# Three-stage chain on one core: steps of the second block on other tiles, a difference of x behind the last low part, one conversion fewer behind a product

## The chip, the cores and the metric

The kernel runs on one core of a Trainium2 chip. The metric is device time in microseconds (us). Before the change three runs gave a median of 1089.61 us, with 1087.82 as the lowest and 1091.75 as the highest.

## The reference

Three stages follow each other; the output of one is the input of the next.

```python
# 1: retention, 4 x 8 heads, 768 steps, head size 64
state = gamma * state + outer(k[t], v[t]);  y[t] = scale * q[t] @ state
x = y as 3072 tokens x 512
# 2: first MLP, w_in 512 x 2048, w_out 2048 x 512
h = maximum(x @ w_in, 0);  x = (h * h) @ w_out
# 3: second MLP, w_gate and w_val 512 x 1536, w_out 1536 x 512
xn = x / sqrt(mean(x * x) + 1e-6) * rms_g
out = (silu(xn @ w_gate) * (xn @ w_val)) @ w_out
```

All of it is float32 on the outside.

## The kernel before, in words

A product of two float32 matrices is made of three TensorE passes over operands that are split in two: a high part (ScalarE casts to fp32r, L105, L339, L488) and a low part (VectorE subtracts the high part from the value, L102). The weights of the later token blocks are used in the form of seven combinations of their four quarters (P1 to P7), so that seven products stand for eight. Such a combination is called a unit here: VectorE adds or subtracts quarters (`plus`, L112, and `sub`, L109), `put` splits the result into high and low part, and SyncE's queue stores it to device memory (L162, `ui` for w_in and `uo` for w_out), from where a ring of tiles fetches it again (L441, `more_ring` and its like).

The 3072 tokens go through the kernel in blocks of 512. Blocks 0 and 1 use the plain weights; block 1 is the **second block** that the change speaks of (`block1(1, ...)`). It walks over 16 tiles f = 0 to 15 of the hidden size. In each tile TensorE multiplies x by w_in (`proj`, L323), ScalarE makes relu, its square and the high part (r L336, r L337, s L339), VectorE makes the low part of s (L102), and TensorE multiplies s by w_out one tile later (`tail1`, `out1`, L281 to L283). On every even tile TensorE also does a **visit** of the retention: one chunk of 128 tokens, with the products for the state and the values (L982, L993, L1002) and the scores of the next chunk (L947). A visit needs q of the next chunk multiplied by its decay on GpSimd (`decay_q`, L924), and q comes from device memory just before (L902).

After block 1 blocks 2 and 3 run as one pair with the combined weights; the pair goes over groups n of four hidden tiles, and over the products k in each group in the order P1, P2, P6, P5, P7, P3, P4 (`after1(n, k)` is called behind each product; visits are behind P6 and P3). The operands of x for these products are made by `first_x` from raw x (three `sub` of 128x1024 and seven `put`).

Three generators are advanced by hand with `next()`, one step at a time, at fixed tiles:

- `made` makes the units of w_out: two steps that add high and low part of four tiles again (`whole_rows`), then `plus` and `sub`, `put(P5)`, `sub` with `put(P7)`, `sub` with `put(P6)`, `put(P3)`.
- `made_in` makes the units of w_in in the same way.
- `coming_xs` is `first_x`.

Beside them a **tick** takes one tile of a later weight of stage 3 a step further: ScalarE unpacks a raw tile into f (L232, L235), VectorE finishes it (L246), SyncE stores the tile before (L205) or a low part is made, and SyncE fetches the next raw tile (L221, 512 KB). `more_steps` opens this list and fetches the first three raw tiles; in block 1 it is called in `last1` at f = MORE_AT.

Nothing is scheduled by a tool: the order of the program's calls is the order on each engine. Within one tile of block 1 that order is `early1`, the background step, `proj`, r/r/s on ScalarE, `late1`, the visit, the mask on VectorE (L965, L970), the low part of s, `after_visit` (copies L314, state L112 and L1013, loads of q, k and v), the decays on GpSimd, `last1`, and `tail1`. All DMAs shown here are issued by SyncE in that order. Working tiles come from one pool of 38 slots (`slot()`), so a write into a slot waits for the last use of it, and that use can be the store of an earlier unit.

Of the kernel before, what the change touches and what calls it, by code (L numbers as in the profile page):

```python
# [35 lines left out]
NF1, NF2 = FF1 // 128, FF2 // 128  # L36
# [4 lines left out]
COMING = (0, 1, 2, 5, 8, 9, 13, 16, 17, 18, 19, 20)  # L41
AHEAD = 5
EARLY = 24
MORE_AT = 6
W2_SOON = 25
X_AT = (11, 12, 17, 18, 23, 24)

P2, P1, P5, P6, P7, P3, P4 = range(7)
# [12 lines left out]
def retention_then_two_mlps(  # L61
# [27 lines left out]
    def slot(name, dt=F32):  # L89
        return wp.tile([128, 2, 512], dt, tag="w", name=name)  # L90

    def big(name, dt=F32):
        return xp.tile([128, KC, TB], dt, tag="x", name=name)
# [10 lines left out]
    def split(dst_h, dst_l, src, el):  # L104
        nc.scalar.copy(dst_h, src)  # L105
        low(el, dst_l, src, dst_h)

    def sub(out_, a, b, eng=nc.vector):
        eng.tensor_tensor(out=out_, in0=a, in1=b, op=ALU.subtract)  # L109
# [144 lines left out]
    def stores():  # L254
        while later:
            later.pop(0)()

    def tick(low_first=False, ahead=True):
        i = at[0]
        rest_of = None  # L260
        if i - 1 in done:
            fn, key, _ = steps[i - 1]
            rest_of = fn(key, done.pop(i - 1))
        if i < upto[0]:
            magnitude(i)
            if ahead:
                magnitude(i + 1)
        if low_first and rest_of:
            rest_of()
        if i < upto[0]:  # L270
            convert(i)
            at[0] = i + 1
        if not low_first and rest_of:
            rest_of()

    def more_steps(n):
        upto[0] = min(upto[0] + n, len(steps))
        fetch_to(at[0] + 2)
# [50 lines left out]
    def background():  # L329
        for w in back[:]:  # L330
            if next(w, StopIteration) is StopIteration:
                back.remove(w)
# [259 lines left out]
    def first_x(raws):  # L592
        y = {(h, t): raws[t].t[:, 2 * h:2 * h + 2, :] for h in range(2) for t in range(2)}

        def put(k, src, wide=False):
            if wide:
                t = big("xop", F32R)
                X[k] = [t[:, 0:2], t[:, 2:4]]
            else:
                X[k] = [slot("xop", F32R) for _ in range(2)]  # L600
            split(*X[k], src, nc.vector)

        yield
        put(P1, y[0, 0])
        yield
        put(P2, y[1, 0])
        yield
        put(P3, y[1, 1])
        yield
        sub(y[0, 0], y[0, 1], y[0, 0])  # L610
        sub(y[0, 1], y[1, 1], y[0, 1])
        yield
        sub(y[1, 1], y[1, 1], y[0, 0])
        yield
        put(P6, y[1, 1])
        yield
        put(P5, y[0, 0])
        yield
        put(P7, y[0, 1], True)
        yield  # L620
        sub(y[1, 0], y[1, 0], y[1, 1])
        put(P4, y[1, 0], True)
        yield
# [242 lines left out]
    with tc.manual_schedule():  # L866
# [92 lines left out]
        def mask(first=0):  # L959
            if not masks:  # L960
                return
            P, sc = masks.pop()
            for h in (first, 1 - first):
                o, i = (a.rearrange("p (g e) i -> p g e i", g=2)[..., D:] for a in (P[:, h], sc[h]))
                nc.vector.tensor_tensor(  # L965
                    out=o, in0=i, in1=seen_sb[:, :, D:].unsqueeze(2).to_broadcast([128, 2, 2, D]), op=ALU.mult
                )
                for n, b in enumerate(heads):
                    g = slice(2 * n, 2 * n + 2)
                    nc.vector.tensor_tensor(  # L970
                        out=P[b, h, g, :D], in0=sc[h][b, g, :D],
                        in1=seen_sb[b, n, :D].unsqueeze(1).to_broadcast([D, 2, D]), op=ALU.mult,
                    )
# [54 lines left out]
        def visit(c, next_banks, with_sums, also=None):  # L1028
            kv = into_state(c)
            kv0 = into_state(also, pr[0]) if also else None  # L1030
            if with_sums:
                sums(pr[0][:, 2 * C:])
            values(c, halves())
            scores(c + 1, next_banks)
            return kv, kv0

        def after_visit(c, x, kv):
            x.put(columns_of(c), halves())
            take_state(c, kv)
            load(c + 2)  # L1040
            load_q(c + 2)
            load_k(c + 2)
            load_v(c + 2)
# [140 lines left out]
        def tail1():  # L1184
            nonlocal prev
            if prev is None:
                return
            pf, s, pj = prev
            prev = None
            out1(pf, s)  # L1190
            if pf == NF1 - 1:
                back.append(norm1(pj, 2 + 2 * pj))
                next(back[-1])
# [76 lines left out]
        def keep_out(f):  # L1270
            keep_units(uo, f, W[("o", f)])

        def keep_in(f):
            q, r, m = f // 4, f % 4 // 2, f % 2
            w = W[("i", f)].bitcast(F32)
            for k, h in ((P1, 0), (P2, 1)) if r == 0 else ((P4, 1),):
                nc.sync.dma_start(units(ui[q][k])[:, m], w[:, :, h * HALF:(h + 1) * HALF])
# [32 lines left out]
        coming_xs = None  # L1310

        def sink1(c):
            nonlocal coming_xs
            t = c // B - 2
            if t == len(raws1):
                raws1.append(Raw())
                if t:
                    coming_xs = first_x(raws1)
                    next(coming_xs)
            return raws1[t]  # L1320

        def early1(f):
            if f in (1, 2, 3, 4, 5, 6, 7, 9, 13):
                next(made)
            if f == NF1 - 1:
                next(coming_xs)

        def late1(f):
            if f + NF1 - 5 < NF1:
                keep_out(f + NF1 - 5)  # L1330
            if f + 4 < NF1:
                keep_in(f + 4)
            if f == NF1 - 1:
                next(coming_xs)
            if f % 2 and 1 < f < NF1 - 1:
                next(made_in)
            elif f == 1:
                next(made)

        def more_ring():  # L1340
            n = len(ring)
            ring.append(slot(f"ring{n}", F32R))
            nc.sync.dma_start(ring[n].bitcast(F32), stream[n])
# [3 lines left out]
        def last1(f):  # L1347
            stores()
            if f >= RING_AT:
                more_ring()  # L1350
            if f < 8 or f in (12, 13):
                next(made)
            if f == MORE_AT:
                more_steps(W2_SOON)
            if f > MORE_AT and f % 2:
                tick(ahead=False)
            if 2 <= f < NF1 - 1:
                next(made_in)
            if f in (8, 10, 14, 15):
                next(coming_xs)  # L1360

        block1(1, cur, sink1, (0, 2, 4, 6, 8, 10, 12, 14), early1, late1, last1)
        stores()
        making_1 = chain(made_in, made)
# [3 lines left out]
        def sink2(c):  # L1368
            t = c // B - 4
            if t == len(xs2):  # L1370
                xs2.append(Raw())
            return xs2[t]
# [18 lines left out]
        def next_chunk():  # L1391
            nonlocal at_chunk
            decay_v(at_chunk + 1, nc.gpsimd)
            decay_q(at_chunk + 2, nc.gpsimd)
            at_chunk += 1

        def after1(n, k):
            if (n, k) == (0, P1):
                tail1()
            else:  # L1400
                background()
            mask()
            stores()
            at_step = k in (P2, P5, P4) or (n, k) == (2, P1)
            if at_step:
                tick(ahead=False)
            if k == P5 or k == P4 and n < NQ - 1:
                next_chunk()
            if k in (P6, P3):
                kv, _ = visit(at_chunk, (ph, pb)[(n + 1) % 2] if k == P6 else pa, True)  # L1410
                after_visit(at_chunk, sink2(at_chunk), kv)
            if at_step:
                next(making_1, None)
            if n == 0 and k in (P1, P2, P6):
                next(coming_xs)
            if (n, k) == (0, P1):
                more_ring()
            if n == NQ - 1 and k in (P2, P6, P3):
                i = (P2, P6, P3).index(k)
                out_1.hi(i)  # L1420
                out_1.lo(i)

        for n in range(NQ):
            in_pair(n, after1)
# [318 lines left out]
```

## Time and profile before

| what | value |
| --- | --- |
| median of three runs | 1089.61 us (1087.82 to 1091.75) |
| the profiled execution's own time | 1087.85 us |
| its span in the profile | 1086.1 us |
| granted TensorE clock, mean | 1.000 of full speed |
| busy share: PE, DVE, ACT, POOL | 99%, 72%, 55%, 7% |

The profile gives the busy time of each engine: PE is TensorE's matmuls, DVE VectorE, ACT ScalarE, POOL GpSimd and SPq SyncE's queue, which issues the DMAs. Times inside the trace count from the start of the span. The span is 1.75 us shorter than the execution's own time. Since PE is busy for 99% of it, the time is that of TensorE's work and of the few places where it waits.

### The profile page before, as it was taken

Reading aid. Unit: us, or ns where it says so; the run is one execution under the profiler, and the core shown is the slowest. Engines: PE = TensorE matmul, PEld = TensorE weight load, DVE = VectorE, ACT = ScalarE, POOL = GpSimd, SP = SyncE. Lnnn points to the kernel's source line nnn. Section 1 sums busy time; section 2 is a strip of 40 time slices with the busy share of each in tenths; the row PEclk is TensorE's granted clock in tenths of the full one; section 3 lists DMA queues with packets and bytes.
Section 4 is the critical chain, followed back from the end, with each engine's and each line's share of the span. In section 5 each row is a group of like instructions: output and inputs, shape, how many; then the busy total and the mean of one; then the engine's idle time right before and its main releaser. Section 6 shows DMA issues by size and latency. Waiting matters only on the chain. (4 is left out here: it accounts for less than half of the span.)

```text
span 1086.1 us, 16642 instructions
## 1 busy us (share of the span) xinstructions
PE 1075.8 (99%) x6257; PEld 883.8 (81%) x6257; DVE 785.3 (72%) x1078; ACT 592.5 (55%) x913; POOL 74.3 (7%) x65
## 2 busy tenths in 40 slices
PE   9999999999999999999999999999999999999998
PEld 7788887878878788888887887888888888888887
DVE  6988698796758995579788887995333896433585
ACT  5777445667677649885465555453333554233442
POOL 3000142214210000000000000000000000000000
PEclk9999999999999999999999999999999999999999
DMA  9979899999999979987669979767567667555563
GB/s 362 339 241 354 260 319 354 383 388 405 344 372 353 348 273 384 388 271 239 200 227 335 378 280 364 263 212 238 194 230 253 194 212 252 194 194 194 194 213 117
DMA packets 110180, 307.16 MB, mean 283 GB/s; under 512 B 11236, under 2 KB 34556, under 8 KB 110100
## 3 DMA queue, kind: packets, MB, share of 16 engines
q1 hardware_dynamic: 109920, 305.85, 79.1%
q8 instruction: 50, 0.82, 0.3%
q10 hardware_dynamic: 180, 0.24, 0.1%
q14 instruction: 30, 0.25, 0.1%
HBM read 217.43 MB, written 88.62 MB: 282 GB/s over the span
## 5 line engine op out<-in xcount | busy, mean ns | idle before, releaser
L488 ACT CAST o<-act 128x1024 fp32r<-128x1024 f32 x101 | 105.6, 1052 | 110.1 <-DVE act L109 50.1
L102 DVE TENSOR_TENSOR o<-act,o 128x1024 fp32r<-128x1024 f32 x101 | 123.0, 1222 | 26.6 <-ACT o L488 26.5
L282 PE MATMUL ph<-o,ring 128*128 128x512 f32 x228 | 88.8, 389 | 0.0
L281 PE MATMUL ph<-o,ring 128*128 128x512 f32 x228 | 88.5, 388 | 0.0
L283 PE MATMUL ph<-o,ring 128*128 128x512 f32 x228 | 88.5, 388 | 0.0
L109 DVE TENSOR_TENSOR act<-act 128x1024 f32<-128x1024 f32 x68 | 83.0, 1221 | 0.3
L281 PE MATMUL ph<-xop,ring 128*128 128x512 f32 x208 | 81.5, 392 | 0.8 <-ACT part L116 0.7
L281 PE MATMUL pb<-xop,ring 128*128 128x512 f32 x208 | 81.4, 391 | 0.4 <-ACT part L116 0.3
L281 PE MATMUL pa<-xop,ring 128*128 128x512 f32 x208 | 81.4, 391 | 0.0
L323 PE MATMUL ph<-xh,w_i 128*128 128x512 f32 x248 | 81.0, 390 | 0.0
L283 PE MATMUL pb<-xop,ring 128*128 128x512 f32 x208 | 81.0, 389 | 0.0
L282 PE MATMUL ph<-xop,ring 128*128 128x512 f32 x208 | 81.0, 389 | 0.0
L283 PE MATMUL pa<-xop,ring 128*128 128x512 f32 x208 | 80.9, 389 | 0.0
L283 PE MATMUL ph<-xop,ring 128*128 128x512 f32 x208 | 80.9, 389 | 0.0
L282 PE MATMUL pb<-xop,ring 128*128 128x512 f32 x208 | 80.9, 389 | 0.0
L282 PE MATMUL pa<-xop,ring 128*128 128x512 f32 x208 | 80.9, 389 | 0.0
L112 DVE TENSOR_TENSOR part<-pr,part 128x512 f32<-128x512 f32 x38 | 25.7, 689 | 52.5 <-ACT part L116 51.2
L760 ACT ACTIVATE t<-part 128x512 f32<-128x512 f32 x54 | 34.1, 632 | 50.0 <-DVE part L112 50.0
L116 ACT COPY part<-ph 128x512 f32<-128x512 f32 x52 | 29.9, 588 | 52.3 <-PE ph L283 52.3
L323 PEld LDWEIGHTS ph<-xh,w_i 128*128 128x128 f32 x248 | 46.5, 188 | 10.2 <-ACT w_o L136 0.4
L282 PEld LDWEIGHTS ph<-o,ring 128*128 128x128 f32 x228 | 42.8, 188 | 9.6 <-DVE o L102 0.9
L281 PEld LDWEIGHTS ph<-o,ring 128*128 128x128 f32 x228 | 42.8, 188 | 9.1 <-issue 0.2
(251 smaller groups left out, 2597.7 us busy)
## 6 DMA issues: line engine op xcount, KB each, us to landing
ring<-wu SPq DMA_DIRECT2D x84, 512.0 KB, 3.9
ring<-up SPq DMA_DIRECT2D x63, 512.0 KB, 4.3
ring<-ui SPq DMA_DIRECT2D x56, 512.0 KB, 6.6
ring<-uo SPq DMA_DIRECT2D x56, 512.0 KB, 4.9
wu<-ring SPq DMA_DIRECT2D x42, 512.0 KB, 7.0
raw<-w1i SPq DMA_DIRECT2D x16, 512.0 KB, 6.9
raw<-w1o SPq DMA_DIRECT2D x16, 512.0 KB, 6.9
vkt<-vk SPq DMA_DIRECT2D x16, 512.0 KB, 7.1
```

The costliest lines, as they stand in the source:

```text
L102: eng.tensor_tensor(out=dst_l, in0=src, in1=dst_h.bitcast(F32), op=ALU.subtract)
L109: eng.tensor_tensor(out=out_, in0=a, in1=b, op=ALU.subtract)
L112: eng.tensor_tensor(out=out_, in0=a, in1=b, op=ALU.add)
L116: nc.scalar.copy(dst[:, m], acc[m])
L281: nc.tensor.matmul(acc, ah, bh, start=start, stop=False, **more)
L282: nc.tensor.matmul(acc, ah, bl, start=False, stop=False, **more)
L283: nc.tensor.matmul(acc, al, bh, start=False, stop=stop, **more)
L323: nc.tensor.matmul(h, w[:, a, k * 128:(k + 1) * 128], x[b][k], start=n == 0, stop=n == len(order) - 1)
L488: nc.scalar.copy(h, src)
L760: nc.scalar.activation(t, g, AF.Silu)
```

## The change

Five places are edited, all in the order of the work; the arithmetic is the same.

```diff
-MORE_AT = 6
+MORE_AT = 4
...
 # first_x
         sub(y[1, 1], y[1, 1], y[0, 0])
-        yield
         put(P6, y[1, 1])
...
         def early1(f):
-            if f in (1, 2, 3, 4, 5, 6, 7, 9, 13):
+            if f in (0, 1, 2, 5, 6, 7, 11, 12, 13):
                 next(made)
...
 # late1
-            if f == NF1 - 1:
-                next(coming_xs)
...
 # last1
             if f > MORE_AT and f % 2:
                 tick(ahead=False)
-            if 2 <= f < NF1 - 1:
+            if 1 <= f < NF1 - 2:
                 next(made_in)
...
 # after1
             at_step = k in (P2, P5, P4) or (n, k) == (2, P1)
-            if at_step:
+            if at_step and k != P1:
                 tick(ahead=False)
```

Three steps of `made` move (from f = 3, 4 and 9 to f = 0, 11 and 12), all steps of `made_in` in `last1` come one tile earlier, the first raw tiles are fetched two tiles earlier and a tick is added at f = 5, the third difference of x leaves the f = 15 code ahead of the low part, and the tick behind the third group's first product goes. The number of steps and of ticks over the whole kernel is the same. From the third group's second product on, the order on all engines is that of before.

Below, rows are shown as they stand in program order on one engine, before and now. Line numbers of the changed kernel are one lower from L614 on.

**ScalarE, second block, from the square of tile 5 to that of tile 6** (r_1988 and r_1992 are tile 5's relu, r_2042 and r_2054 tile 6's; made tiles are units). Before:

```order
L337 ACTIVATE r_1988<-r_1988 128x512 [waits Activation_49]
L339 CAST s_1991<-r_1988 128x512 [waits DMAHW1_49,Activation_49]
L105 CAST made_1996<-rows_1803 128x2x256
L105 CAST made_2006<-rows_1850 128x2x256 [waits DVE_49]
L105 CAST made_2010<-sm_1854 128x2x256 [waits DVE_49,PE_49]
L105 CAST made_2026<-sm_1950 128x2x256 [waits DVE_49]
L336 ACTIVATE r_2042<-ph0_230 128x512 [waits PE_49]
```

Now:

```order
L337 ACTIVATE r_1992<-r_1992 128x512 [waits Activation_49]
L339 CAST s_1995<-r_1992 128x512 [waits Activation_49]
L105 CAST made_2000<-sm_1846 128x2x256 [waits DVE_49]
L105 CAST made_2008<-sm_1976 128x2x256 [waits DMAHW1_49,DVE_49]
L232 ACTIVATE rows_2015<-raw_1954 128x512 [waits DMAHW2_49]
L235 ACTIVATE raw_1954<-raw_1954 128x512 [waits DMAHW4_49]
L105 CAST made_2022<-rows_1707 128x2x256 [waits DMAHW0_49,DVE_49]
L105 CAST made_2038<-rows_1853 128x2x256 [waits DVE_49]
L336 ACTIVATE r_2054<-ph0_230 128x512 [waits PE_49]
```

The four casts ahead of tile 6's relu are still four, the added tick puts L232 and L235 among them, and the third cast, made_2022, now also waits for a DMA: its slot is the one that made_2000 had, and the DMA is the store of made_2000 (`ui03<-made_2000`).

**VectorE, second block, tile 5, between the state's addition and the mask of tile 6.** Now:

```order
L112 TENSOR_TENSOR rows_1854<-w_o6_895 128x512 [waits DMAHW7_49]
L112 TENSOR_TENSOR rows_1854<-w_o7_944 128x512
L109 TENSOR_TENSOR sm_1846<-sm_1846,rows_1707 128x512 [waits DVE_49]
L102 TENSOR_TENSOR made_1961<-rows_1708,made_1961 128x2x256 [waits Activation_49]
L112 TENSOR_TENSOR sm_1976<-rows_1853,rows_1854 128x512 [waits DMAHW1_49,DVE_49]
L109 TENSOR_TENSOR rows_1853<-rows_1853 128x2x256 [waits DVE_49]
L109 TENSOR_TENSOR rows_1707<-rows_1707,sm_1846 128x2x256
L102 TENSOR_TENSOR made_2000<-sm_1846,made_2000 128x2x256 [waits PE_49,Activation_49]
L102 TENSOR_TENSOR s_1995<-r_1992,s_1995 128x512
```

Before, six instructions of the same size stood between the state's addition and tile 5's low part of s; now eight do, the last of them the low part of made_2000. Between the state's addition of the visit before (f = 2) and the mask of f = 4 there were 14 such instructions and are nine now.

**VectorE, second block, tile 15** (raw is x for `first_x`, xop its split operands). Before, and behind it now:

```order
L102 TENSOR_TENSOR xop<-raw,xop 128x1024
L109 TENSOR_TENSOR raw<-raw 128x1024 x3
L102 TENSOR_TENSOR s<-r,s 128x512
L102 TENSOR_TENSOR wps<-rows,wps 128x512
L246 SCALAR_TENSOR_TENSOR f<-f,raw 128x512
L102 TENSOR_TENSOR xop<-raw,xop 128x1024
```

```order
L102 TENSOR_TENSOR xop<-raw,xop 128x1024
L109 TENSOR_TENSOR raw<-raw 128x1024 x2
L102 TENSOR_TENSOR s<-r,s 128x512
L246 SCALAR_TENSOR_TENSOR f<-f,raw 128x512
L109 TENSOR_TENSOR raw<-raw 128x1024
L102 TENSOR_TENSOR xop<-raw,xop 128x1024
```

The third difference moved from ahead of the low part of s to behind it.

## Rows read from the trace of the kernel before

**Rows 1.** The page, part 1: busy time, share, instructions of each engine.

```profile
PE 1075.8 (99%) x6257; PEld 883.8 (81%) x6257; DVE 785.3 (72%) x1078; ACT 592.5 (55%) x913; POOL 74.3 (7%) x65
```

**Rows 2.** PE's waits: line, what ended them, us in total, times, longest.

```profile
PE ph L947 <- issue: 1.7, 1, 1.7
PE pa L947 <- POOL qnt L924: 1.3, 2, 1.1
...
PE pa L282 <- DVE s L102: 0.9, 1, 0.9
```

**Rows 3.** Timeline of PE, scores of f = 2, 4, 6: start, us.

```profile
135.93 0.85 PE L947 MATMUL ph<-qnt,kTt 64*64 64x128 f32 x32
...
149.79 0.85 PE L947 MATMUL ph<-qnt,kTt 64*64 64x128 f32 x32
...
165.49 0.72 PE L947 MATMUL ph<-qnt,kTt 64*64 64x128 f32 x19 [1.65 <-issue]
```

**Rows 4.** Timeline of ACT ahead of the scores of f = 6.

```profile
164.28 0.62 ACT L105 CAST made<-sm 128x512 fp32r<-128x512 f32 x1 [2.22 <-DVE sm L109]
164.80 0.59 ACT L336 ACTIVATE r<-ph 128x512 f32<-128x512 f32 x1
```

**Rows 5.** Timeline of DVE from the visit of f = 2 to f = 6.

```profile
139.82 0.68 DVE L109 TENSOR_TENSOR rows<-rows,sm 128x512 f32<-128x512 f32 x1
...
151.84 0.42 DVE L965 TENSOR_TENSOR causal<-ph,seen_sb 128x256 f32<-128x256 f32 x1
...
154.46 0.42 DVE L112 TENSOR_TENSOR st<-st,pr 128x256 f32<-128x256 f32 x1
...
156.42 3.23 DVE L102 TENSOR_TENSOR made<-sm,made 128x512 fp32r<-128x512 f32 x2
...
162.96 0.68 DVE L102 TENSOR_TENSOR s<-r,s 128x512 fp32r<-128x512 f32 x1
163.57 0.68 DVE L109 TENSOR_TENSOR sm<-sm,rows 128x512 f32<-128x512 f32 x1
```

**Rows 6.** Timeline of POOL there: the first and the last of five instructions.

```profile
155.02 0.93 POOL L1013 TENSOR_TENSOR st<-st,sdec_sb 128x256 f32<-128x256 f32 x1 [9.19 <-DVE st L112]
...
160.76 1.73 POOL L398 TENSOR_TENSOR y<-y 128x512 f32<-128x512 f32 x1
```

**Rows 7.** DMA issues at 159.7 and at 163.1: KB, us to landing.

```profile
uo<-made SPq DMA_DIRECT2D x1, 512.0 KB, 4.5
...
ui<-made SPq DMA_DIRECT2D x1, 512.0 KB, 2.6
```

**Rows 8.** Stretches: us, engines' busy times, granted clock, DMA share, GB/s.

```profile
162.00:164.00 2.00, 1.84 (x46) 1.43 (x40) 2.00 (x3) 0.06 (x1) 0.49 (x1) 1.00 0.37 147
164.00:168.00 4.00, 2.51 (x39) 2.21 (x40) 3.99 (x9) 3.66 (x8) 0.00 (x0) 1.00 0.87 268
...
216.00:284.00 68.00, 66.85 (x635) 54.47 (x634) 52.12 (x85) 45.92 (x74) 20.40 (x17) 1.00 1.03 395
```

**Rows 9.** Timeline of DVE at f = 15.

```profile
229.18 4.84 DVE L109 TENSOR_TENSOR raw<-raw 128x1024 f32<-128x1024 f32 x3
233.93 0.69 DVE L102 TENSOR_TENSOR s<-r,s 128x512 fp32r<-128x512 f32 x1
```

**Rows 10.** Timeline of PE at f = 15.

```profile
234.67 0.50 PE L282 MATMUL pa<-s,w_o 128*128 128x512 f32 x1 [0.95 <-DVE s L102]
```

**Rows 11.** Timeline of POOL: the two q decays that PE waits for.

```profile
255.02 1.27 POOL L924 TENSOR_TENSOR qnt<-qnt,qdec_sb 128x512 f32<-128x512 f32 x1 [5.78 <-DMA qnt<-qT]
...
306.01 1.26 POOL L924 TENSOR_TENSOR qnt<-qnt,qdec_sb 128x512 f32<-128x512 f32 x1 [16.54 <-DMA qnt<-qT]
```

**Rows 12.** Timeline of SyncE's queue ahead of the second of them.

```profile
292.10 0.80 SPq L221 DMA_DIRECT2D raw<-w2g  x1
...
297.33 0.47 SPq L902 DMA_DIRECT2D qnt<-qT  x1
```

**Rows 13.** DMA issue at 297.33: KB, us to landing.

```profile
qnt<-qT SPq DMA_DIRECT2D x1, 256.0 KB, 8.5
```

## The prediction

> **What bounds the kernel now.** Read the busy times first: TensorE works for 99% of the span [rows 1], so its work sets the end, and an edit that only moves the work of other engines counts where TensorE waits for them. Then read TensorE's waits [rows 2]. Four of them lie where the change is at work, and I call them A to D: A is the scores of tile 6 in the second block (1.7 us, put down to "issue"); B is the product of tile 15's s, which waits for its low part (0.9 us); C and D are the scores behind GpSimd's decay of q (1.3 us in two waits, the longer 1.1 us, so 0.2 us and 1.1 us). Third, read the starts of the scores [rows 3]: from tile 2 to 4 it is 13.86 us, from 4 to 6 it is 15.70 us. So A costs 1.84 us for 1.65 us of idle, as the pipeline also drains and fills. I add the same 0.2 us to the other waits: B 1.15 us, C 0.4 us, D 1.3 us. All four together are 4.7 us, 0.43% of 1089.6 us. That is the most the change can win. About 0.3%, here 3.3 us, is what a measurement of this kernel can tell from no change.
>
> **A: steps of the units on other tiles, and one tick more.** What ends A is hidden behind the word "issue". The scores of tile 6 overwrite the bank that ScalarE's relu reads; that relu starts at 164.80 and takes 0.59 us, and the scores start 0.10 us later. Ahead of it on ScalarE stands a cast of a unit that had waited 2.22 us for VectorE [rows 4]. VectorE was late since instructions with two inputs in SBUF took 1.6 us each (3.23 us for two) while GpSimd was at work, from 155.02 to 162.49 [rows 6], and 0.61 us from start to start behind that, 162.96 to 163.57 [rows 5].
>
> The change shuffles this. VectorE now has nine instructions instead of 14 between the visit of tile 2 and the mask of tile 4. Before, these ran without a pause from 139.82 to 151.84 [rows 5], while the scores had ended at 150.64 (149.79 + 0.85, [rows 3]). So the mask can come up to 1.2 us earlier, and the state's addition and GpSimd's five instructions with it. Behind the state's addition VectorE then has eight instructions ahead of tile 5's low part instead of six. The six ended at 162.96; 1.2 us earlier, and with two more at 0.61 us, the eighth ends at 163.0. This eighth is the low part of made_2000, and here a new wait starts. The third cast ahead of tile 6's relu, made_2022, goes into the slot of made_2000, so it waits until the store of made_2000 has landed. In the kernel before no cast near here stood so close behind the store of its slot.
>
> That store can be issued at 163.05. Two stores of this size next to it landed 4.5 and 2.6 us after their issue [rows 7]. I take 3.0 us, near the quicker one: that one was issued at 163.07, when the DMA engines were busy for only 0.37 of the time [rows 8]. Landing is then 166.05. Behind it come two casts, 0.52 us each from start to start (164.28 to 164.80), the relu of 0.59 us and 0.10 us [rows 4], together 1.73 us: the scores start at 167.8 instead of 165.49, **2.3 us later than before**, in place of a gain. Bounds: if VectorE is a further 1.0 us sooner (one of its instructions escapes GpSimd) and the store takes 2.6 us, 0.9 us; if the mask comes no earlier (164.2 in place of 163.0) and the store takes 4.5 us, 5.0 us. A gain at A is excluded as long as this wait holds, since an undelayed start at 163.65 would need the store landed by 161.9, before made_2000 is complete.
>
> [...]
>
> The other casts of the added tick cost nothing on TensorE's path: L232 and L235 stand ahead of the cast that waits longer. The step of `made` at tile 0 and the earlier `made_in` at tile 1 fall where TensorE waits for nothing; if that cover were gone, a step there would cost its own cast and subtraction, 0.5 to 0.7 us [rows 4, 5].
>
> **B: the third difference behind the low part.** Three differences took 4.84 us, 1.61 us each, and the low part of s followed at 233.93 [rows 9]. With one fewer ahead of it, it starts at 232.3 and ends at 233.0, 0.5 us before TensorE asks (234.67 less 1.1 us, [rows 10]). **Gain 1.15 us**; bounds 0 and 1.15. The difference itself now stands in front of the operand P6, which the pair uses only in its third product; that cover is long.
>
> **C: q's decay at 255.** GpSimd waited 5.78 us for the load of q there [rows 11], in a stretch where the DMA share is 1.03 [rows 8]. So its time is set by bytes, not by the order of the engines. The added tick brings a store of 0.26 MB and a fetch of 0.52 MB ahead of it, 0.79 MB, at 395 GB/s [rows 8] 2.0 us, partly into idle time such as 162 to 164 (share 0.37). TensorE comes 2.3 - 1.15 = 1.15 us later, more than the 0.4 us. I take **a gain of 0.4 us**; bounds that and a loss of 0.85 us (2.0 less 1.15).
>
> **D: the tick behind the third group's first product.** The load of q issued at 297.33 took 8.5 us [rows 13], against 2.6 us for one of twice the bytes in a quiet stretch [rows 7]; the difference is queue. Its removed tick stood in this queue: a store and the fetch issued at 292.10 [rows 12], again 0.79 MB, 2.0 us at 395 GB/s. That is more than D's 1.3 us. **Gain 1.3 us**; bounds 0 (the DMA engines idle while SyncE waits for its next issue) and 1.3. What is late next there is nothing that I see.
>
> **Sum:** 2.3 - 1.15 - 0.4 - 1.3 = -0.55 us. The profiled execution took 1087.85 us and would take 1087.3 us; it lies 1.76 us below the median of the runs, so the median goes from 1089.61 to **1089.1 us**. Its own range, with the bounds of A and half of those of B to D, is 1087.5 to 1092 us.
>
> **The rivals.**
> - *The slot costs nothing and the gains come.* If the cast's wait is over when ScalarE gets there, A shrinks: only the two casts and the relu are left behind L235, and about 1.2 of its 1.84 us go. With B, C and D that is -4.0 us, 1085.6 us. For it: GpSimd and VectorE finish sooner. Against it: the store cannot land before 2.6 us have passed.
> - *The clock falls at A (slower).* TensorE would stand idle from 163.65 to 167.8, some 4 us, over twice the longest wait of before (1.65 us), behind which the granted clock stayed at 1.00 [rows 3, 8]. [...] It decides if the idle time at A reaches some 4 us. [...]
> - *The store lands late.* With A at its upper bound, 5.0 us, the sum is +2.15, and +3.45 if D also stays: 1091.8 to 1093.1 us.
> - *DMA sets the pace.* If A loses little, the gains at A and B are given back at C, as q's load comes at the same time whatever TensorE does; only D is left: 1088.3 us.
>
> **How the numbers follow.** The forecast gets 0.50, the free slot 0.20, the clock 0.13, the late store 0.09, the DMA 0.08. Faster by over 0.3% are the free slot and a little of the forecast's spread: 0.21. Slower are the clock and half of the late store: 0.18. The rest, 0.61, is within 0.3%. The range, 1085.8 to 1093.8 us, takes in the bounds of the unknown terms and leaves out half of the free slot's cases below and the worse half of the clock's above.
>
> **What would show it.** Right: TensorE's wait ahead of tile 6's scores grows from 1.65 to some 4 us, with ScalarE's third cast waiting for a DMA `ui<-made`; the waits on the low part of s at tile 15 and on q's decay at 255 and 306 are gone; the granted clock stays at 1.00. Wrong: scores of tile 6 that start before 165.5 (A's step falls), a wait at 306 of over 0.5 us (D's falls), a granted clock below 1.00 behind tile 6 (the clock's rival holds), or a new wait of TensorE in tiles 0 to 4.

## The result and the profile after

The changed kernel takes 1095.97 us (median of five executions, 1094.5 to 1098.44) against 1089.32 us (five, 1087.82 to 1091.75): ratio 1.0064, interval 1.0043 to 1.0085. It is slower by about 7 us. The profiled execution took 1095.37 us with a span of 1093.7 us and a mean granted clock of 0.998; the other four had 0.994 to 0.998, where the profiled execution of before had 1.000.

TensorE's busy time on the page of the changed kernel, against [rows 1]:

```profile
PE 1077.4 (99%) x6257; PEld 885.6 (81%) x6257; DVE 783.1 (72%) x1078; ACT 592.8 (54%) x913; POOL 74.9 (7%) x65
```

The other engines did the same work, and TensorE was busy 1.6 us longer for the same 6257 matmuls. TensorE's waits after, against [rows 2]:

```profile
PE ph L946 <- issue: 5.8, 2, 4.4
PE pa L946 <- POOL qnt L923: 2.1, 1, 2.1
...
PE pa L282 <- DVE ol L102: 1.1, 1, 1.1
```

The wait on tile 15's low part of s is gone, and of the two on q's decay one is left, larger. But "issue" now stands for two waits. They are in the timeline of TensorE, against [rows 3]; the third row is the wait for q:

```profile
138.72 0.90 PE L946 MATMUL ph<-qnt,kTt 64*64 64x128 f32 x32 [1.39 <-issue]
...
171.12 1.19 PE L946 MATMUL ph<-qnt,kTt 64*64 64x128 f32 x19 [4.42 <-issue]
...
264.16 0.90 PE L946 MATMUL pa<-qnt,kTt 64*64 64x128 f32 x32 [2.07 <-POOL qnt L923]
```

TensorE's order is the same in both kernels, so the start of every matmul can be compared with that of its twin. The steps in which the difference grows or shrinks, each read where the difference has settled, are the account of the two profiled executions (us); three smaller ones behind 500 (-0.4, -0.3 and +0.5) nearly cancel:

| where | step |
| --- | --- |
| ahead of 32, before the first edit acts | +1.2 |
| scores of tile 2 | +1.6 |
| scores of tile 6 | +2.8 |
| the 7 us behind them | +1.6 |
| tile 15's product | -1.2 |
| scores at q's load (255 before, 264 after) | +1.9 |
| the state's product at 276 | +0.3 |
| scores at q's load (306 before, 313 after) | -1.4 |
| o's low part at 371 | +0.7 |
| sum | +7.5 |

**Tile 6** went as the prediction says. ScalarE there, against [rows 4]:

```profile
163.15 0.62 ACT L105 CAST made<-sm 128x512 fp32r<-128x512 f32 x1 [1.50 <-DVE sm L112]
163.67 0.66 ACT L232 ACTIVATE rows<-raw 128x512 f32<-128x512 f32 x1
164.24 0.68 ACT L235 ACTIVATE raw<-raw 128x512 int32<-128x512 uint8 x1
169.39 1.14 ACT L105 CAST made<-rows 128x512 fp32r<-128x512 f32 x2 [4.47 <-DMA ui<-made]
170.43 0.59 ACT L336 ACTIVATE r<-ph 128x512 f32<-128x512 f32 x1
```

VectorE there, against [rows 5]:

```profile
165.35 0.68 DVE L102 TENSOR_TENSOR made<-sm,made 128x512 fp32r<-128x512 f32 x1
```

The low part of made_2000 ends at 166.03. The cast that needs its slot starts 3.4 us later, at 169.39, and the row names the DMA `ui<-made` as what it waited for. Then come two casts, the relu and the scores at 171.12.

**The clock.** The stretches around it, with the granted clock in the third column from the right, against [rows 8]:

```profile
168.00:170.00 2.00, 0.00 (x0) 0.00 (x0) 0.00 (x0) 0.61 (x2) 0.00 (x0) 1.00 1.03 248
170.00:172.00 2.00, 0.88 (x19) 0.91 (x22) 1.90 (x3) 1.94 (x5) 0.00 (x0) 0.80 0.94 258
172.00:174.00 2.00, 2.00 (x24) 1.61 (x19) 1.24 (x4) 1.40 (x4) 0.00 (x0) 0.50 1.01 387
174.00:176.00 2.00, 2.00 (x9) 1.62 (x8) 1.92 (x6) 0.00 (x0) 0.08 (x1) 0.84 1.03 376
```

TensorE did nothing in 168 to 170; behind it the granted clock is 0.80, 0.50 and 0.84 in stretches of 2 us, and 1.00 again from 176 to 178. The products of s, one 128x512 matmul each, start 0.43 us apart at 0.50 (173.16, 173.59, 174.02), against 0.23 us at 1.00 (175.00, 175.23, 175.46). What the three stretches lack of the full clock comes to 1.7 us (0.40 + 1.00 + 0.32), an estimate that is near the 1.6 us of the table.

**Tile 2** is a wait that the prediction did not have. ScalarE there:

```profile
136.47 0.62 ACT L105 CAST made<-sm 128x512 fp32r<-128x512 f32 x1 [2.77 <-DVE rows L112]
137.00 1.14 ACT L395 ACTIVATE y<-y 128x512 f32<-128x512 f32 x2
138.05 0.58 ACT L336 ACTIVATE r<-ph 128x512 f32<-128x512 f32 x1
```

A cast of the w_out units, which comes here because of the step at tile 0, waits for VectorE's addition of a w_in row: the cast's slot was that of w_in's first tile, and this addition, moved one tile earlier, is that tile's last reader. Two squares and the relu follow, and the scores behind them.

**Tile 15.** VectorE, against [rows 9]:

```profile
233.91 3.62 DVE L109 TENSOR_TENSOR raw<-raw 128x1024 f32<-128x1024 f32 x2
237.46 0.68 DVE L102 TENSOR_TENSOR s<-r,s 128x512 fp32r<-128x512 f32 x1
```

The low part ends at 238.14, and the second matmul starts at 240.75 without a wait.

**q's load at 255.** The last product of the visit ahead of the load on TensorE, and the load's issue on SyncE's queue, before:

```profile
244.33 0.67 PE L1002 MATMUL pr<-qnt,st 64*64 64x128 f32 x16
246.67 1.45 SPq L902 DMA_DIRECT2D qnt<-qT  x1
```

And now, with GpSimd's decay, against [rows 11]:

```profile
250.27 0.67 PE L1001 MATMUL pr<-qnt,st 64*64 64x128 f32 x16
253.78 0.33 SPq L901 DMA_DIRECT2D qnt<-qT  x1
262.84 1.27 POOL L923 TENSOR_TENSOR qnt<-qnt,qdec_sb 128x512 f32<-128x512 f32 x1 [7.65 <-DMA qnt<-qT]
```

The program issues the load behind that visit. The visit's product starts 5.9 us later, the issue ends 6.0 us later (at 254.11 instead of 248.12), and the decay starts 7.8 us later: 8.7 us pass between issue and decay instead of 6.9.

### The profile page after: what moved, and what is told of

Read it like the earlier page. It is cut to its first block, busy times and chain, and to the rows that moved or that the text cites. A ratio compares the mean times of both kernels' runs of the same rounds, so it can differ in the third digit from the quotient of the medians.

```text
span 1093.7 us, 16656 instructions
## 1 busy us (share of the span) xinstructions
PE 1077.4 (99%) x6257; PEld 885.6 (81%) x6257; DVE 783.1 (72%) x1078; ACT 592.8 (54%) x913; POOL 74.9 (7%) x65
```

## The experiments

In each, the parts not named are those of the kernel that it starts from. A ratio is to the kernel before on the same chip; intervals are 95%.

**One part of the change alone: the third difference** (on the kernel before)

```diff
         sub(y[1, 1], y[1, 1], y[0, 0])
-        yield
         put(P6, y[1, 1])
...
-            if f == NF1 - 1:
-                next(coming_xs)
```

> The kernel before with the third difference alone behind the low part of s. Theory (each edit acts at one place): tile 15's product no longer waits, 1.1 us less, nothing else changes: ratio 0.999. Rival (the gain is given back at q's load at 255, which comes at the same time whatever TensorE does): the wait there grows from 0.2 to about 1.3 us and the time stays within 0.3 us.

Ratio 1.0001 (0.9988 to 1.0013). Its waits on q:

```profile
PE pa L946 <- POOL qnt L923: 2.3, 2, 1.6
```

Tile 15's product comes 1.2 us earlier against its twin, and the scores at 255 step back by 1.4 us: their idle time grows from 0.2 to 1.6 us. The rival holds for the time: the gain at tile 15 is given back at the state's product behind it (0.7 us) and at q's load (1.4 us).

**One part alone: the steps of both unit generators** (on the kernel before)

```diff
-            if f in (1, 2, 3, 4, 5, 6, 7, 9, 13):
+            if f in (0, 1, 2, 5, 6, 7, 11, 12, 13):
...
-            if 2 <= f < NF1 - 1:
+            if 1 <= f < NF1 - 2:
```

> The kernel before with the moved steps of both unit generators alone (early1's list and the range of made_in). Slot theory: the casts ahead of tile 6's relu wait for no store in flight, as the raw tiles don't hold slots yet, so tile 6's scores come up to 1.1 us earlier than before; tile 2's scores stall by about 1.6 us as in the changed kernel (the cast of a unit waits for a tile whose reader on VectorE is late); tile 15's wait goes, as two VectorE instructions less stand ahead of it: in sum -0.6 us, granted clock 1.00. Rival (the moved steps themselves cause the wait of tile 6): a stall of 3 to 4.4 us at tile 6 here too, and +4 us or more.

Ratio 1.0043 (1.0028 to 1.0059). Tile 2's stall is there (+1.65 us against the twin), tile 6's shrinks (-1.2 us, idle time 0.48 us), tile 15's goes (-1.2 us), all three as the theory said. What it did not have is a new stall at tile 8, +2.6 us:

```profile
181.64 0.66 ACT L232 ACTIVATE rows<-raw 128x512 f32<-128x512 f32 x1 [6.75 <-DMA raw<-w2o]
```

The tick of tile 7 waits for a raw tile that is only fetched from tile 6 on, and tile 8's relu stands behind it. The stretch behind this idle time of 2.45 us runs at a lower clock too:

```profile
184.00:188.00 4.00, 4.00 (x30) 3.17 (x23) 3.85 (x11) 2.63 (x5) 0.00 (x0) 0.60 1.03 398
```

So the moved steps do not make the stall of tile 6. They make that of tile 2, and with raw tiles fetched from tile 6 one at tile 8 (the change fetches from tile 4, and has none there).

**One part alone: the tick** (on the kernel before)

```diff
-MORE_AT = 6
+MORE_AT = 4
...
-            if at_step:
+            if at_step and k != P1:
```

> The kernel before with the tick alone moved (MORE_AT 4, none behind the third group's first product). Slot theory: the three raw tiles and two row tiles taken two tiles earlier leave few slots, and two casts ahead of tile 6's relu now wait for stores issued just before, so the stall of tile 6 grows from 1.65 us to 2.5 to 4.5 us; the wait at 255 grows by 1 to 2 us with the 0.79 MB moved ahead of it, the one at 306 goes (-1.3 us): +1 to +5 us in sum, more if the clock falls. Rival (the wait comes from the moved steps): tile 6's stall stays within 0.7 us of before, and the sum is within 1 us of before.

Ratio 1.0030 (1.0017 to 1.0043). TensorE's waits:

```profile
PE ph L947 <- issue: 4.6, 1, 4.6
PE pa L947 <- POOL qnt L924: 2.7, 1, 2.7
...
PE pa L282 <- DVE s L102: 0.8, 1, 0.8
```

Tile 6 stalls as long as in the changed kernel, without any moved step; against the twins its scores step by +3.0 us, those at 255 by +2.5 us, those at 306 by -1.4 us, and TensorE loses 1.3 us more behind the first and 1.6 us more behind the second idle stretch, which I put down to the clock (mean 0.997 in this execution, 1.000 before). But the stall is made up otherwise than in the changed kernel. ScalarE ahead of tile 6's relu:

```profile
162.36 0.62 ACT L105 CAST made<-rows 128x512 fp32r<-128x512 f32 x1 [2.84 <-DVE made L102]
164.16 0.66 ACT L232 ACTIVATE rows<-raw 128x512 f32<-128x512 f32 x1 [1.19 <-DVE made L102]
166.50 0.62 ACT L105 CAST made<-sm 128x512 fp32r<-128x512 f32 x1 [0.61 <-DMA uo<-made]
```

In the program's allocation the first two write into slots that hold rows which VectorE's low parts still have to read, and only the last waits for a store, for 0.6 us. So the length of the stall agrees with the expectation, its two waits for stores do not: here slots that VectorE frees late make most of it.

**The slot alone: two stores in another place** (on the changed kernel)

```diff
         def last1(f):
-            stores()
+            if f != 5:
+                stores()
...
                 next(made_in)
+            if f == 5:
+                stores()
```

> The changed kernel, with the stores of tile 5 issued behind that tile's tick and unit step instead of ahead of them, so that the third cast gets the slot of the unit before (whose store was issued 4.6 us earlier and landed 1.6 us earlier). All engines keep their work and order, only two stores change places in the queue. Slot theory: tile 6's scores come about 1.6 us earlier, the idle time falls from 4.4 to about 2.8 us, and the granted clock stays at 1.00 (1.6 us more): about 3 us less than the changed kernel. Rival (the added tick's own work on ScalarE and VectorE makes the stall): no change.

Ratio 1.0088 (1.0062 to 1.0114): it went the other way. ScalarE and SyncE's queue:

```profile
172.59 0.62 ACT L105 CAST made<-rows 128x512 fp32r<-128x512 f32 x1 [8.76 <-DMA ui<-made]
```

```profile
166.76 0.33 SPq L221 DMA_DIRECT2D raw<-w2o  x1
167.14 0.91 SPq L162 DMA_DIRECT2D ui<-made  x2
```

The cast did get the slot of the unit before, but behind the tick's loads, one of which SyncE could issue only at 166.76, that unit's store was issued at 167.14 instead of 161.44. The idle time grew from 4.4 to 9.6 us. My size was wrong since I left out what stands ahead of the stores in the queue; the verdict on the theories is clear all the same: the compute engines' work and order are unchanged, and the stall grew by 5 us, of which about 4 us are the later landing of the store and 0.8 us the next cast's wait for VectorE. The tick's work on ScalarE and VectorE alone does not set it.

**The relu ahead of the casts** (on the changed kernel)

```diff
-            if f in (0, 1, 2, 5, 6, 7, 11, 12, 13):
+            if f in (0, 1, 2, 5, 7, 11, 12, 13):
...
+            if f == 6:
+                next(made_in)
+                next(made)
...
-            if 1 <= f < NF1 - 2:
+            if 1 <= f < NF1 - 2 and f != 5:
```

> The changed kernel, with the two unit steps whose casts stood ahead of tile 6's relu behind the added tick (the one that waited for the store among them) issued behind the relu and its square. Slot theory: tile 6's scores no longer wait for the store, their idle time falls from 4.4 us to under 0.7 us, the granted clock stays at 1.00 there (4.4 + 1.6 us less), and one to three of these 6 us come back as a longer wait at q's load (2.1 us in the changed kernel): 3 to 5 us less than the changed kernel, about 1091 to 1093 us. Rival (the added tick's work and the DMA bytes make the stall): idle time at tile 6 stays above 3 us.

Ratio 1.0055 (1.0040 to 1.0071), 1094.68 us. Tile 6's scores start without a wait, 4.6 us earlier against the twin in the changed kernel. But the slot of made_2000 now falls to the next in line, the high part of tile 6's s:

```profile
168.94 0.62 ACT L339 CAST s<-r 128x512 fp32r<-128x512 f32 x1 [3.93 <-DMA ui<-made]
```

The mask stands behind it on VectorE, and the next product waits for the mask:

```profile
PE ph L323 <- DVE causal L969: 3.8, 1, 3.8
PE pa L946 <- POOL qnt L923: 3.0, 1, 3.0
```

The wait moved to the next instruction that takes the slot, and most of its price stayed; the clock fell behind both of these waits (0.86 from 170 to 175 and 0.79 from 175 to 180, 0.74 from 260 to 265 and 0.58 from 265 to 270). By the ratios 1 us is gained, not the 3 to 5 us expected.

**More free slots** (on the changed kernel: one raw tile fetched at f = 4 and one by tile 5's tick)

```diff
-        fetch_to(at[0] + 2)
+        fetch_to(at[0] + (2 if n != W2_SOON else 0))
...
-        fetch_to(i + AHEAD if i + AHEAD < EARLY else max(i + 3, EARLY - 1))
+        fetch_to(i + AHEAD if i + AHEAD < EARLY else max(i + (1 if lean[0] else 3), EARLY - 1))
...
+            lean[0] = f == 5
```

> The changed kernel, but one raw tile instead of three is fetched at f = 4 and one instead of two more by the added tick's end, so that two slots more are free at tile 6. Order and work of ScalarE and VectorE are those of the changed kernel, up to the fetches. Slot theory: made_2022's step gets a slot without a store in flight, and its neighbour waits for a store issued 4.6 us earlier with 1 MB less ahead of it; tile 6's idle time falls from 4.4 us to 0.3 to 1.5 us, and the granted clock stays at 1.00 there; some of it comes back at q's load: 2 to 5 us less than the changed kernel, 1091 to 1094 us. Rival (the tick's own work on ScalarE and VectorE): idle time of over 3 us stays.

Ratio 1.0010 (0.9996 to 1.0024), 1089.36 us: some 6 us of the loss are gone, more than the 2 to 5 us expected. ScalarE and VectorE keep their order and the tick its work; TensorE's waits are

```profile
PE pa L947 <- POOL qnt L924: 2.8, 1, 2.8
PE ph L947 <- issue: 1.9, 2, 1.4
```

with 1.4 us at tile 2 and 0.54 us at tile 6, where the clock stays at 1.00 from 163 to 170. ScalarE's third cast no longer waits for a DMA:

```profile
163.73 1.14 ACT L105 CAST made<-rows 128x512 fp32r<-128x512 f32 x2 [0.59 <-DVE rows L109]
```

In the program's allocation its slot is now one whose last use is a product of TensorE. This settles tile 6 of the changed kernel: the stall is the slot that the early fetches leave for the cast. The 0.7 us by which the wait at q's load is longer than in the changed kernel, and the clock that falls behind it (0.68 from 254 to 262) and costs 2.8 us in the profiled execution, are what comes back.

**As that, without the step at tile 0** (it stays at tile 9)

```diff
-            if f in (0, 1, 2, 5, 6, 7, 11, 12, 13):
+            if f in (1, 2, 5, 6, 7, 9, 11, 12, 13):
```

> As a_lean, with the w_out units' step of tile 0 back at tile 9. Theory for the new stall at tile 2 (1.4 us of idle time): the step of tile 0 puts one cast more ahead of tile 2's relu, and that cast waits for a slot that VectorE frees late; without it the stall falls to 0.7 us or less, 1 us less than a_lean. Rival (the earlier w_in steps alone put VectorE behind): the stall at tile 2 stays above 1.2 us.

Ratio 1.0002 (0.9987 to 1.0017). The idle time at tile 2 falls from 1.39 to 0.44 us, as the theory said: the step at tile 0 makes two thirds of that stall; the earlier w_in step is the only other edit ahead of it and so makes the rest. Tile 6 is back at 1.77 us, but not for a slot: the steps of `made` come one later, and the last cast ahead of the relu waits for VectorE's sum.

```profile
164.25 0.62 ACT L105 CAST made<-sm 128x512 fp32r<-128x512 f32 x1 [1.19 <-DVE sm L112]
```

The time is not told apart from that of the run before.

**q's load ahead of a tick's bytes** (on the kernel before)

```diff
-            if at_step:
+            if at_step and k != P2:
                 tick(ahead=False)
...
                 after_visit(at_chunk, sink2(at_chunk), kv)
+            if k == P6:
+                tick(ahead=False)
```

> The kernel before with one thing moved: the ticks behind each group's second product now come behind the visit that follows the third, so that a visit's load of q stands ahead of their store and fetch (0.79 MB) in the queue. Theory (q's load is late because of the bytes ahead of it): the loads land about 2 us earlier, the waits of 0.2 us at 255 and of 1.1 us at 306 go, 1.7 us less in sum: ratio 0.9984. Rival (the loads are late by their own start or by the following loads): the waits stay.

Both waits on q are gone from TensorE's list, as expected, but the ratio is 1.0000 (0.9988 to 1.0013). In the profiled execution the granted clock fell behind tile 6's unchanged stall (1.70 us of idle time):

```profile
166.00:170.00 4.00, 4.00 (x29) 3.12 (x22) 3.88 (x10) 2.20 (x5) 0.00 (x0) 0.57 0.89 289
```

Four of its ten executions had a clock of 0.998, and five of 27 of the kernel before. The gain was not lost to that alone: the other executions have a median of 1087.5 us in both kernels. Against the twins the scores at 306 gain 1.4 us, and 1.0 us comes back between 250 and 258, where a product at 252.95 and the scores wait anew (0.2 us each).

**Tile 6's step behind the relu** (on the kernel before, where no slot is short)

```diff
-            if f in (1, 2, 3, 4, 5, 6, 7, 9, 13):
+            if f in (1, 2, 3, 4, 5, 7, 9, 13):
...
-            elif f == 1:
+            elif f == 1 or f == 6:
                 next(made)
```

> The kernel before with tile 6's step of the w_out units behind that tile's relu and nothing else. Theory: tile 6's stall goes (1.65 us of idle time), and with it the runs in which the granted clock falls behind it (0.998 in 6 of 23 runs of the kernel before); the wait at 255 grows by what TensorE gains there, so that the time is within 1 us of before (ratio 0.999 to 1.000). Rival (the gain stays): ratio 0.998.

Ratio 0.9990 (0.9977 to 1.0002), 1087.72 us, within the expectation. Against the twins tile 6's scores gain 1.9 us; 1.0 us comes back at the next product, which now waits for the mask, and 1.0 us at 255. Two of its twelve executions still had a clock of 0.998, against eight of 35 of the kernel before, so the falls became fewer at most and did not go.

**All of it together, on the kernel before:** the last two edits and the third difference

```diff
-            if f in (1, 2, 3, 4, 5, 6, 7, 9, 13):
+            if f in (1, 2, 3, 4, 5, 7, 9, 13):
...
-            elif f == 1:
+            elif f == 1 or f == 6:
...
         sub(y[1, 1], y[1, 1], y[0, 0])
-        yield
...
-            if f == NF1 - 1:
-                next(coming_xs)
...
-            if at_step:
+            if at_step and k != P2:
...
+            if k == P6:
+                tick(ahead=False)
```

> The kernel before with the ticks moved as in the run b_p2, the third difference behind the low part, and tile 6's step of the w_out units behind that tile's relu. Theory: the stalls at tile 6 (1.85 us) and at tile 15 (1.1 us) go, the one at 306 goes (1.3 us), and at 255 TensorE comes 3 us earlier than before while q's load comes 2 us earlier, so that some 1.4 us stay: 3 us less in sum, ratio 0.997. Rival (q's load at 255 is fixed by the DMA bytes of the whole stretch from 216 on, not by those just ahead of it): the gains of tiles 6 and 15 come back there in full, and the ratio is 0.9985 or more.

**The same, with tile 15's tick behind the first visit of the pair**

```diff
-            if f > MORE_AT and f % 2:
+            if f > MORE_AT and f % 2 and f < NF1 - 1:
...
             if k == P6:
                 tick(ahead=False)
+            if (n, k) == (0, P6):
+                tick(ahead=False)
```

> As b_all, with the tick of tile 15 also moved behind the first visit of the following pair, so that 0.79 MB more stand behind q's load at 255. Theory (bytes ahead of q's load set it): the remaining 1.4 us at 255 go as well: 4 us less than before, ratio 0.996. Rival (fixed by something else): like b_all.

These two beat both kernels: ratios 0.9985 (0.9975 to 0.9994) and 0.9982 (0.9973 to 0.9991), 1086.19 and 1085.78 us against 1087.93 us. The first has no wait on q in its list any more. Two of the larger waits left there are

```profile
PE pa L282 <- DVE ol L102: 0.8, 1, 0.8
PE ph L323 <- DVE causal L969: 0.7, 1, 0.7
```

Its scores of tile 6, tile 15's product and the scores at 306 gain 1.9, 1.2 and 1.4 us against their twins. The profiled execution ends 1.4 us ahead of that of before, but 0.8 us of this lie ahead of the first edit, so that it keeps 0.6 of the 4.5 us: 1.0 us returns at the mask, 0.6 at 240, 0.6 at 255, the rest further on. The medians are 1.7 us apart, half of what I expected. The ratio is that of the rival, but its mechanism is not what the trace shows, since the gains of tiles 6 and 15 did not come back in full at 255. None of the 21 executions of the two runs had a clock below 0.999, against five of 27 of the kernel before. The other 22 of the 27 have a median of 1087.5 us, so that 1.3 of the 1.7 us stay without the clock. The two intervals don't tell the second step from the first, which is its rival.

**The moved ticks in the changed kernel with more free slots** (with the step at tile 9)

```diff
-            if at_step and k != P1:
+            if at_step and k not in (P1, P2):
...
+            if k == P6:
+                tick(ahead=False)
```

> a_lean1 with the ticks of the second product behind the visit after the third (as in b_p2): all four waits of the kernel before are addressed as the change meant to, without its slot wait. Theory: 3 us less than before if no wait takes their place, ratio 0.997; rival (the 0.79 MB of the added tick ahead of 255 cost what the moved ticks gain): ratio 0.999 to 1.001.

Ratio 0.9998 (0.9985 to 1.0010): the rival. The waits of tile 6 (1.8 us) and tile 2 (0.4 us) are there, and 0.7 us at q's scores. In the profiled execution the clock fell behind the wait at tile 6 (0.57 from 166 to 170).

## Why the prediction was wrong

Three steps failed: the price of the tick's bytes at q's load (C), the steps at tiles 0 and 1 that were put at nothing, and the clock, which was left out of the sum. The rest held.

- *Tile 6 (A)* was right in cause and near in size: 2.3 us forecast, 2.8 us measured. The low part of made_2000 was forecast at 163.0, and at TensorE's delay of 2.9 us there it ended at 163.2 (166.03 - 2.9); the landing was forecast 3.0 us behind its issue and the cast started 3.4 us behind the low part. The 0.2 us that I added to each wait has the right size (tile 2 stepped by 1.6 us for 1.39 us of idle time); that it is the pipeline that drains and fills is my estimate.
- *The step that missed by most* is C, q's load at 255: "its time is set by bytes, not by the order of the engines". I took a gain of 0.4 us, with a loss of 0.85 us as the bound, and it lost 1.9 us. I let TensorE's delay cover the bytes of the added tick, as if the load came at a time of its own. But the load is issued behind a visit and came later with it: TensorE was 5.9 us late there, the issue 6.0 us, and the load then took 8.7 us to the decay in place of 6.9. The run with the tick alone lost 2.5 us there although TensorE was 3.7 us late. The 1.8 us are near the 2.0 us of the moved bytes, but with the third difference alone, which moves no bytes, the load took 8.2 us as well (its issue ended at 247.30, the decay began at 255.49); which part the bytes have stays open.
- *The step that was put at nothing* is "the step of `made` at tile 0 and the earlier `made_in` at tile 1 fall where TensorE waits for nothing". I priced the lost cover at 0.5 to 0.7 us; it was 1.6 us. The slot rule that I followed for tile 6 holds at tile 2 as well: the cast of tile 0's extra step waits for the last reader of w_in's first tile, which VectorE reached only when TensorE was about to ask.
- *The clock* was a rival with a chance of 0.13 and belongs to the forecast. I set its weight by the one idle stretch of 1.65 us that had kept the clock. By the rows a stretch of 4 us stands outside all that the trace showed, and the price of a fall should have been part of the term A. The upper end of the forecast's range took in a price of a fall that no run shows; in the profiled execution the fall cost 1.6 us. Three of the other four executions had a lower mean clock (0.994 to 0.997 against 0.998); what that cost no trace shows.
- *Tile 15 (B) and 306 (D)* were right: 1.2 and 1.4 us gained in the changed kernel. Alone, B's gain came back at the state's product behind it and at 255 (the third difference alone, ratio 1.0001); the part at 255 is the rival in which DMA sets the pace.
- In sum: A + 2.8, B - 1.2, C + 1.9, D - 1.4, and the two that the forecast left out, tile 2 + 1.6 and the clock + 1.6, make + 5.3 us of the 7.5 us between the profiled executions; 1.2 us more lie ahead of the first edit, the rest at 276 and 371. The forecast had -0.55 us. Its own range of 1087.5 to 1092 us is also narrower than its bounds: A's upper bound and half of B's to D's, added to 1089.1, give 1093.6 us.

## What to carry to other kernels

An instruction that makes the next tile of a pool waits for the last use of the slot that it gets, and that can be a store still in flight (here ScalarE stood idle for 4.47 us ahead of such a cast); before tiles are loaded earlier, count the slots that they hold, and look at what stands behind each write into a just freed slot on its engine. Where an engine in order has to do something for TensorE, put it ahead of work for later, and check where the wait lands then (with tile 6's relu ahead of the casts its scores came 4.6 us earlier, and the next product waited 3.8 us). A gain ahead of a stretch in which the DMA engines are full (share 1.03 from 216 to 284) can be given back at the load that ends it, as with the third difference alone (1.4 us at 255), and a delay there can grow at it (5.9 us at the visit, 7.8 us at the decay in the changed kernel); look first at what that load is issued behind.

## What the runs showed of the hardware

A short idle stretch of TensorE can cost more than its own length: behind the 4.42 us at tile 6 of the changed kernel another 1.6 us were lost. In the profiled executions the granted clock stayed at 1.00 behind idle stretches of 1.65 us (before), 1.77 us (the run without the step at tile 0) and 2.07 us (after, at 264), and fell behind 1.70 us (the run with q's load moved, 0.57 over the next 4 us), 1.78 us (the moved ticks in the changed kernel, 0.57 over 4 us), 2.45 us (both generators' steps alone, 0.60 over 4 us), 4.4 us (after, 0.50 from 172 to 174) and 9.6 us (the two stores in another place, 0.50 from 174 to 180). So length alone does not tell between 1.7 and 2.1 us, and what does no run here shows. What I put down to one fall is 1.3 to 2.8 us against the twins. In the kernel before the clock falls in some executions too: among its 23 beside the first experiments, 17 had a mean clock of 1.000 with a median of 1087.8 us, and six had 0.998 with 1090.6 us.
